# A two-layer Strassen kernel on one core: the first product in five groups of 464 token pairs instead of six of 384

## The chip, the core and the metric

The kernel runs on one core of a Trainium2 chip. The metric is the device time of one execution in microseconds, the median of several runs. Engines: TensorE (PE; its weight loads PEld), VectorE (DVE), ScalarE (ACT), GpSimd (POOL) and SyncE (SP), which here only issues DMAs.

## The reference

Chunked attention feeds two feed-forward layers in a row, all in float32:

```python
scores = scale * (q_c @ k_c.T)                 # chunks of 64 tokens, 8 heads of 64
x = softmax(scores) @ v_c                      # 4608 tokens x 512
h = x @ w_in;  s = h * softmax(h)              # first layer, 1024 wide
y = (layernorm(s) * g_ln) @ w_out              # 4608 x 512
h = y @ w_in2                                  # second layer, 2048 wide
g = max(h, 0) + alpha * min(h, 0)
out = g @ w_out2                               # 4608 x 512
```

## The kernel before

The first phase computes attention and the first layer for 36 tiles of 128 tokens, in an order written out by hand (`FIRST`, `STEP`, `LAST`), and stores `y` transposed to DRAM, one tensor `y_dram[s]` for each group of tokens (`ystore`, stores issued by SP, for the last two blocks by ACT).

The second phase, `phase2`, computes the second layer as two products, each with Strassen's scheme in its form of seven products of halves. Tokens go in pairs (first half, second half of a group), 2304 pairs in all. Each float32 operand is split into a high part (`high_y`, ACT) and a low part (`low_y`, DVE), and a product of halves takes three matmuls for each of two row blocks: six matmuls of one `w_in2` weight block each.

First product: six groups `s` of `SG` = 384 pairs, and for each group eight units `b`, one for each pair of 128 columns of the hidden layer. A unit runs the products p1, p6, p5, p7, p2, p3, p4, 42 matmuls with 384 columns. They go to four PSUM banks, x, y, z and v; p2, p3 and p4 add to the banks x, z and v after `s1` (ACT) has read x, `w` (DVE, output `wv`) has read z and `f("22")` has read v. Units take two sets of four banks in turn. DVE and ACT compute the four results of a unit (`f`, then `neg`, `pos`, and `end`, which together are the activation) and SP stores each, `g`, to DRAM (`gd`). The last three steps of a unit (`late`) are issued among the products of the next one.

The operands of the first product lie in 26 slots of one size on the left of SBUF. A group holds 14 while it runs: a high and a low part for each of seven products. During group `s` the next group is prepared: its four blocks of `y` are loaded at unit 1 (`load_y`, SP), the four sums are made by POOL at units 2 to 4 (`sum_y`), and the high and low parts follow at the places in `early`, `(unit, product)`: the low part always one product behind. A slot is taken from the top or from the bottom of the free ones, in turn by group. Where it stands in a unit: `extra(k)` is called after the k-th product has been issued with what reads it, so `(7, 1)` is in unit 7 behind p6 and what `late(2)` stores.

Second product: five chunks of pairs (`CHUNKS`); a chunk takes 28 steps of 12 matmuls, over four pieces `j`; first the products p1, p5, p6, p7 of all four pieces, then p2, p3, p4. A piece loads blocks a, b, c, d of `g` (`load_g`), and DVE and ACT make sums and parts (`prepare`, three steps ahead). Pieces 0 and 1 are prepared during the last group, in the same slots; their sums t4 go through DRAM. All later pieces use other buffers (`rp`, `op`, `hp`), which take over the slots' memory from the left end once the slots are given up (`ca.close()`). During the last group SP also loads the second product's weights, a quarter at a time (`load_w`).

Of the kernel before, what the change touches and what calls it, by code (L numbers as in the profile page):

```python
# [22 lines left out]
NT = B * S  # L23
# [10 lines left out]
SG = 384  # L34
NS = NT // (2 * SG)
PAIRS = NT // 2
NB2 = KF2 // 2
CHUNKS = [(0, 384), (384, 512), (896, 512), (1408, 512), (1920, 384)]
# [55 lines left out]
def tile_chunk_attention_solu_prelu(  # L94
# [24 lines left out]
    y_dram = [dram.tile([128, K1, 2 * SG], F32, name=f"yd{j}") for j in range(NS)]  # L119
# [49 lines left out]
    def phase1():  # L169
        with ExitStack() as c1, ExitStack() as c0:  # L170
# [394 lines left out]
            def ystore(j, m):  # L565
# [3 lines left out]
                for c, p in enumerate(pairs):  # L569
                    g, o = divmod(j * YG + p * YP, 2 * SG)  # L570
                    (nc.sync if j < YT + 3 else nc.scalar).dma_start(
                        out=y_dram[g][:, m, o:o + YP], in_=y[:, c * YP:(c + 1) * YP]
                    )
# [99 lines left out]
    def phase2():  # L673
        with ExitStack() as c2:
# [7 lines left out]
            tp = [P(f"t2{i}", 1, stack=ca) for i in range(26)]  # L682
# [13 lines left out]
            slots = list(range(26))  # L696
            homes, at = {}, [True]

            def slot(dtype, name, top=False):
                k = slots.pop(slots.index((max if top else min)(slots)))  # L700
                t = tp[k].tile([128, 2, SG], dtype, name=name, tag="t")
                homes[t.name] = k
                return t

            def free(t):
                slots.append(homes.pop(t.name))
# [3 lines left out]
            def load_y(s, which=YQ):  # L710
                at[0] = s % 2 == 0
                for t in which:
                    r, c = int(t[0]) - 1, int(t[1]) - 1
                    raw[t] = slot(F32 if t == "12" else F32R, f"y{t}", at[0])
                    nc.sync.dma_start(
                        out=raw[t].bitcast(F32), in_=y_dram[s][:, 2 * r:2 * r + 2, SG * c:SG * c + SG]
                    )

            def sum_y(k):
                out, a, b = (("t3", "22", "12"), ("t1", "12", "11"), ("t2", "22", "t1"), ("t4", "21", "t2"))[k]  # L720
                raw[out] = raw["12"] if out == "t1" else slot(F32, f"y{out}", at[0])
                for h in range(2):
                    sub(nc.gpsimd, *(raw[x][:, h].bitcast(F32) for x in (out, a, b)))

            def high_y(s, p):
                t = PRODUCTS[p][1]
                th[s, t] = slot(F32R, "th", at[0])
                copy(th[s, t], raw[t].bitcast(F32))

            def low_y(s, p):  # L730
                t = PRODUCTS[p][1]
                h, f = th[s, t], raw[t]
                l = slot(F32R, "tl", at[0]) if t[0] == "t" else f
# [5 lines left out]
            class Unit:  # L739


                def __init__(self, n, s, b):
                    self.s, self.b = s, b
                    self.ps = {x: ps2[n % 2].tile([128, SG], F32, name=f"h{x}", tag=f"b{x}") for x in "xyzv"}
# [16 lines left out]
                def tile(self, tag, where=None, bufs=1):  # L761
                    return (where or up).tile([128, SG], F32, name=tag, tag=tag, bufs=bufs)
# [33 lines left out]
                def store(self, t):  # L796
                    nc.sync.dma_start(out=GD[t][:, self.b, self.s * SG:self.s * SG + SG], in_=self.g[t])
# [331 lines left out]
```

## Time and profile before

| | |
|---|---|
| median of 3 runs | 1267.35 us (1267.33 to 1267.88) |
| profiled execution | 1267.81 us, of which the span in the trace is 1265.8 us |
| mean granted TensorE clock | 0.992 |
| PE busy | 1227.7 us (97% of the span), 8160 matmuls |
| DVE busy | 935.3 us (74%) |
| ACT busy | 682.5 us (54%) |
| POOL busy | 327.9 us (26%) |
| DMA | 237.89 MB, 188 GB/s on the mean |

The span runs from the first to the last instruction of the trace. Times in the rows are microseconds from the span's start unless marked ns. Matmuls overlap: one of 384 columns lasts 334 ns, but the next starts sooner, so the distance of starts is what counts. A wait is shown as the idle time of an engine and what ended it.

### The profile page before, as it was taken

The numbers are of one execution on the slowest core, as the hardware profiler recorded it, in microseconds if no ns is written. First come the engines' busy times: TensorE is split into PE (matmuls) and PEld (weight loads), VectorE is DVE, ScalarE is ACT, GpSimd is POOL, SyncE is SP. The second block draws the span as 40 slices with busy tenths as digits, with TensorE's granted clock in tenths as the row PEclk, the third lists the DMA queues.
The fourth block names the chain that finished last, engine by engine and source line by source line (L and its number), as shares of the span: only waits on it lengthen the run. The fifth ranks groups of instructions, "written<-read, shape, count | busy, mean of one in ns | idle before, by whom it ended". The sixth has DMA issues, their size and how long they took to land.

```text
span 1265.8 us, 21771 instructions
## 1 busy us (share of the span) xinstructions
PE 1227.7 (97%) x8160; PEld 1102.9 (87%) x8160; DVE 935.3 (74%) x1423; ACT 682.5 (54%) x1140; POOL 327.9 (26%) x309
## 2 busy tenths in 40 slices
PE   5789999999999999999999999999999999999998
PEld 4668888888888888879999999999989888888898
DVE  7986587777877777427878777777876959678584
ACT  6685455555556555436667666576534434434442
POOL 4665155535656545402020211200000000000000
PEclk8899999999999999999999999999999999999999
DMA  8443356554755633559444343428986648274462
GB/s 326 160 148 117 104 167 188 170 189 142 241 183 184 225 135 134 209 183 361 165 147 155 120 150 113 163 100 313 369 307 222 211 138 290 87 271 145 160 223 100
DMA packets 150409, 237.89 MB, mean 188 GB/s; under 512 B 15008, under 2 KB 100512, under 8 KB 149792
## 3 DMA queue, kind: packets, MB, share of 16 engines
q1 hardware_dynamic: 147840, 233.62, 53.9%
q10 hardware_dynamic: 2304, 2.10, 0.5%
q8 instruction: 64, 1.05, 0.3%
q0 software_dynamic: 160, 0.79, 0.1%
q14 instruction: 41, 0.34, 0.1%
HBM read 149.68 MB, written 86.77 MB: 187 GB/s over the span
## 4 chain that ended last, share of the span: by engine, by line
PE 47%; DMA 5%; DVE 1%; issue 0%; SPq 0%; ACT 0%; DVEq 0%; ACTq 0%
PE oz L986 7%; PE ov L986 7%; PE ox L986 7%; PE hz L753 7%; PE hv L753 6%; PE hx L753 6%; PE oy L986 3%; PE hy L753 3%; DMA w<-wod 3%; DMA rc<-gd 1%; DMA gd<-g 0%; DVE rt L668 0%; DVE rb L668 0%; DVE rlo L668 0%; DVE u L665 0%
## 5 line engine op out<-in xcount | busy, mean ns | idle before, releaser
L792 DVE SCALAR_TENSOR_TENSOR g<-ng,nal,g 128x384 f32<-128x384 f32 x192 | 124.1, 647 | 50.5 <-ACT g L671 50.5
L671 ACT ACTIVATE ng<-g 128x384 f32<-128x384 f32 x144 | 75.7, 526 | 119.1 <-DVE g L665 119.1
L165 PE MATMUL yps<-zz,wo_h 128*128 128x512 f32 x288 | 115.2, 400 | 0.8 <-ACT ysb L567 0.8
L753 PE MATMUL hv<-th,w 128*128 128x384 f32 x384 | 112.9, 334 | 1.5 <-DVE g L665 1.5
L753 PE MATMUL hz<-th,w 128*128 128x384 f32 x384 | 112.9, 334 | 0.1
L753 PE MATMUL hx<-th,w 128*128 128x384 f32 x384 | 112.8, 334 | 0.0
L167 PE MATMUL yps<-zz,wo_l 128*128 128x512 f32 x288 | 112.4, 390 | 0.0
L166 PE MATMUL yps<-zz,wo_h 128*128 128x512 f32 x288 | 112.2, 390 | 0.0
L986 PE MATMUL oz<-rhi,w 128*128 128x512 f32 (+1 forms) x304 | 93.9, 369 | 0.8 <-DVE osb L665 0.8
L986 PE MATMUL ox<-rhi,w 128*128 128x512 f32 (+1 forms) x304 | 93.8, 369 | 0.0
L986 PE MATMUL ov<-rhi,w 128*128 128x512 f32 (+1 forms) x304 | 93.7, 369 | 0.0
L668 POOL TENSOR_TENSOR yt<-y,y 128x384 f32<-128x384 f32 x24 | 28.2, 1194 | 235.4 <-DMA y<-yd 136.4
L671 ACT ACTIVATE rhi<-rt 128x1024 fp32r<-128x1024 f32 (+1 forms) x56 | 54.6, 984 | 60.7 <-PE oz L986 16.4
L671 ACT ACTIVATE g<-g 128x384 f32<-128x384 f32 x144 | 75.2, 522 | 3.1
L668 DVE TENSOR_TENSOR rlo<-rt,rhi 128x1024 fp32r<-128x1024 f32 (+1 forms) x56 | 62.3, 1125 | 15.2 <-ACT rhi L671 15.0
L753 PEld LDWEIGHTS hv<-th,w 128*128 128x128 f32 x384 | 70.7, 188 | 1.8 <-DVE g L665 1.8
L753 PEld LDWEIGHTS hz<-th,w 128*128 128x128 f32 x384 | 70.7, 188 | 0.4 <-DVE wv L665 0.4
L753 PEld LDWEIGHTS hx<-th,w 128*128 128x128 f32 x384 | 70.7, 188 | 0.0
L458 PE MATMUL h<-wi_h,xh 128*128 128x512 f32 x256 | 68.9, 391 | 0.0
L458 PE MATMUL h<-wi_l,xh 128*128 128x512 f32 x256 | 68.5, 389 | 0.0
L494 ACT ACTIVATE eh<-sl,st 128x1024 f32<-128x1024 f32 x36 | 41.4, 1151 | 45.5 <-DVE st L489 45.5
L167 PEld LDWEIGHTS yps<-zz,wo_l 128*128 128x128 f32 x288 | 54.0, 188 | 11.7
(179 smaller groups left out, 3270.4 us busy)
## 6 DMA issues: line engine op xcount, KB each, us to landing
gd<-g SPq DMA_DIRECT2D x192, 192.0 KB, 1.9
qkt<-in_qk SPq DMA_DIRECT2D x36, 512.0 KB, 5.6
w<-wod SPq DMA_DIRECT2D x28, 448.0 KB, 6.5
rc<-gd SPq DMA_DIRECT2D x24, 512.0 KB, 3.9
rd<-gd SPq DMA_DIRECT2D x24, 512.0 KB, 4.9
raw<-in_moe_w_out SPq DMA_DIRECT2D x24, 511.8 KB, 4.3
vt<-in_v SPq DMA_DIRECT2D x36, 256.0 KB, 4.5
y<-yd SPq DMA_DIRECT2D x24, 384.0 KB, 5.0
```

Source lines behind the costliest of these rows:

```text
L165: nc.tensor.matmul(o, lh, rh, start=first, stop=False)
L166: nc.tensor.matmul(o, lh, rl, start=False, stop=False)
L167: nc.tensor.matmul(o, ll, rh, start=False, stop=last)
L458: nc.tensor.matmul(ps[:, n], xh[:, kk], w[:, kk, 512 * n:512 * n + 512], start=(kk == 0 and w is wi_h), stop=False,)
L494: nc.scalar.activation(out=e, in_=s, func=AF.Square, bias=st[:, 4:5], accum_out=st[:, 5:6])
L668: eng.tensor_tensor(out=out, in0=a, in1=b, op=ALU.subtract)
L671: nc.scalar.activation(out=out, in_=in_, func=func, **k)
L753: nc.tensor.matmul(self.ps[x], w[:, a, i, k], d[:, k], start=(p not in CHAINED and k + j == 0), stop=(k == 1 and j == 2), skip_group_check ...
L792: nc.vector.scalar_tensor_tensor(out=self.g[t], in0=self.n[t], scalar=nal_sb[:, f:f + 1], in1=self.g[t], op0=ALU.mult, op1=ALU.add)
L986: nc.tensor.matmul(bank[key, m][:, :n], W[2 * j + k][:, a, i, 128 * m:128 * m + 128], d[:, k], start=(p not in CHAINED and j + k + q == 0) ...
```

## The change

The first product runs over five groups, four of 464 pairs and one of 448. A slot holds 464 columns and there are 24. Blocks 22 and 21 of `y` are given up once POOL's last sums have read them, and loaded again in unit 7, where the high and low parts of p2, p3 and p4 now stand two products later. The chunks of the second product are 464, 480, 480, 480 and 400 pairs wide, and its buffers 480. Piece 1 of the second product loads blocks c and d in unit 7. The t4 sums are stored by SP in place of POOL. The SBUF set aside for software DMA is given a size of its own, 512 B a partition. `y` stores are split where they cross a group's border.

```diff
 YP = 256
-SG = 384
-NS = NT // (2 * SG)
 PAIRS = NT // 2
+SG = 464
+GROUP = [(0, 464), (464, 464), (928, 464), (1392, 464), (1856, 448)]
+NS = len(GROUP)
+NSLOT = 24
 NB2 = KF2 // 2
-CHUNKS = [(0, 384), (384, 512), (896, 512), (1408, 512), (1920, 384)]
+CW = 480
+CHUNKS = [(0, 464), (464, 480), (944, 480), (1424, 480), (1904, 400)]
...
     b64 = const.tile([128, 2], F32, name="b64")
-    y_dram = [dram.tile([128, K1, 2 * SG], F32, name=f"yd{j}") for j in range(NS)]
+    y_dram = [dram.tile([128, K1, 2 * n], F32, name=f"yd{j}") for j, (_, n) in enumerate(GROUP)]
...
                 for c, p in enumerate(pairs):
-                    g, o = divmod(j * YG + p * YP, 2 * SG)
-                    (nc.sync if j < YT + 3 else nc.scalar).dma_start(
-                        out=y_dram[g][:, m, o:o + YP], in_=y[:, c * YP:(c + 1) * YP]
-                    )
+                    t0 = j * YG + p * YP
+                    for g, (p0, n) in enumerate(GROUP):
+                        a, b = max(t0, 2 * p0), min(t0 + YP, 2 * (p0 + n))
+                        if a < b:
+                            o = c * YP - t0
+                            (nc.sync if j < YT + 3 else nc.scalar).dma_start(
+                                out=y_dram[g][:, m, a - 2 * p0:b - 2 * p0], in_=y[:, a + o:b + o]
+                            )
...
             ca = c2.enter_context(ExitStack())
-            tp = [P(f"t2{i}", 1, stack=ca) for i in range(26)]
+            tp = [P(f"t2{i}", 1, stack=ca) for i in range(NSLOT)]
             wr = {}
...
-            slots = list(range(26))
+            slots = list(range(NSLOT))
             homes, at = {}, [True]
...
-            def slot(dtype, name, top=False):
+            def slot(dtype, name, top, n):
                 k = slots.pop(slots.index((max if top else min)(slots)))
-                t = tp[k].tile([128, 2, SG], dtype, name=name, tag="t")
-                homes[t.name] = k
+                t = tp[k].tile([128, 2, SG], dtype, name=name, tag="t")[:, :, :n]
+                homes[id(t)] = k, t
                 return t
...
             def free(t):
-                slots.append(homes.pop(t.name))
+                slots.append(homes.pop(id(t))[0])
...
                 at[0] = s % 2 == 0
+                n = GROUP[s][1]
                 for t in which:
                     r, c = int(t[0]) - 1, int(t[1]) - 1
-                    raw[t] = slot(F32 if t == "12" else F32R, f"y{t}", at[0])
+                    raw[t] = slot(F32 if t == "12" else F32R, f"y{t}", at[0], n)
                     nc.sync.dma_start(
-                        out=raw[t].bitcast(F32), in_=y_dram[s][:, 2 * r:2 * r + 2, SG * c:SG * c + SG]
+                        out=raw[t].bitcast(F32), in_=y_dram[s][:, 2 * r:2 * r + 2, n * c:n * c + n]
                     )
...
-            def sum_y(k):
+            def sum_y(s, k):
                 out, a, b = (("t3", "22", "12"), ("t1", "12", "11"), ("t2", "22", "t1"), ("t4", "21", "t2"))[k]
-                raw[out] = raw["12"] if out == "t1" else slot(F32, f"y{out}", at[0])
+                raw[out] = raw["12"] if out == "t1" else slot(F32, f"y{out}", at[0], GROUP[s][1])
                 for h in range(2):
                     sub(nc.gpsimd, *(raw[x][:, h].bitcast(F32) for x in (out, a, b)))
+                if s and k > 1:
+                    free(raw.pop(a))
...
                 t = PRODUCTS[p][1]
-                th[s, t] = slot(F32R, "th", at[0])
+                th[s, t] = slot(F32R, "th", at[0], GROUP[s][1])
                 copy(th[s, t], raw[t].bitcast(F32))
...
                 h, f = th[s, t], raw[t]
-                l = slot(F32R, "tl", at[0]) if t[0] == "t" else f
+                l = slot(F32R, "tl", at[0], GROUP[s][1]) if t[0] == "t" else f
                 sub(nc.vector, l, f.bitcast(F32), h.bitcast(F32))
...
                     self.s, self.b = s, b
-                    self.ps = {x: ps2[n % 2].tile([128, SG], F32, name=f"h{x}", tag=f"b{x}") for x in "xyzv"}
+                    self.p0, self.w_ = GROUP[s]
+                    self.ps = {
+                        x: ps2[n % 2].tile([128, SG], F32, name=f"h{x}", tag=f"b{x}")[:, :self.w_] for x in "xyzv"
+                    }
                     self.g, self.n = {}, {}
...
                 def tile(self, tag, where=None, bufs=1):
-                    return (where or up).tile([128, SG], F32, name=tag, tag=tag, bufs=bufs)
+                    return (where or up).tile([128, SG], F32, name=tag, tag=tag, bufs=bufs)[:, :self.w_]
...
                 def store(self, t):
-                    nc.sync.dma_start(out=GD[t][:, self.b, self.s * SG:self.s * SG + SG], in_=self.g[t])
+                    nc.sync.dma_start(out=GD[t][:, self.b, self.p0:self.p0 + self.w_], in_=self.g[t])
...
             for k in range(4):
-                sum_y(k)
+                sum_y(0, k)
             for p in PRODUCTS:
...
                 if x in pieces[:2]:
-                    return slot(dtype, f"f{tag}", True)
+                    return slot(dtype, f"f{tag}", True, n)
                 bufs = dict(t3=1, t2=1, t4=4, hi=4, lo=3).get(tag, 2)
-                return (hp if tag == "hi" else rp).tile([128, 2, 512], dtype, name=f"r{tag}", tag=tag, bufs=bufs)[:, :, :n]
-
-            def load_g(x):
+                return (hp if tag == "hi" else rp).tile([128, 2, CW], dtype, name=f"r{tag}", tag=tag, bufs=bufs)[:, :, :n]
+
+            def load_g(x, which="abcd"):
                 c, g, j = x
...
                 for tag, t in (("a", "11"), ("b", "12"), ("c", "22"), ("d", "21"))[2 * g:]:
+                    if tag not in which:
+                        continue
                     src[x, tag] = new(x, tag, F32 if tag == "b" else F32R)
...
                 free(d)
-                nc.gpsimd.dma_start(out=t4_dram[x[2]], in_=t4)
                 yield
+                nc.sync.dma_start(out=t4_dram[x[2]], in_=t4)
                 low6()
...
                     if x in pieces[:2]:
-                        nc.gpsimd.dma_start(out=t4_dram[x[2]], in_=t4)
+                        nc.sync.dma_start(out=t4_dram[x[2]], in_=t4)
                         done(t4)
...
                 def new_o():
-                    return op.tile([128, 512], F32, name="osb", tag="osb", bufs=2)[:, :n]
+                    return op.tile([128, CW], F32, name="osb", tag="osb", bufs=2)[:, :n]
...
                     if p == "p1":
-                        acc["u", m] = op.tile([128, 512], F32, name=f"u{m}", tag=f"u{m}")[:, :n]
+                        acc["u", m] = op.tile([128, CW], F32, name=f"u{m}", tag=f"u{m}")[:, :n]
                         copy(acc["u", m], x)
...
-            early = {(4, 1): "p1", (5, 1): "p6", (6, 1): "p5", (6, 2): "p7", (7, 1): "p2", (7, 2): "p3", (7, 3): "p4"}
+            early = {(4, 1): "p1", (5, 1): "p6", (6, 1): "p5", (6, 2): "p7", (7, 3): "p2", (7, 4): "p3", (7, 5): "p4"}
+            again = {(7, 1): ("21",), (7, 2): ("22",)}
             sums = {(2, 0): 0, (2, 3): 1, (3, 0): 2, (4, 0): 3}
...
                             if (b, k) == (6, 5):
-                                load_g(pieces[1])
+                                load_g(pieces[1], "ab")
+                            if (b, k) == (7, 1):
+                                load_g(pieces[1], "cd")
                             if b in (3, 4, 5, 6) and k in (2, 3):
...
                             if (b, k) in sums:
-                                sum_y(sums[b, k])
+                                sum_y(s + 1, sums[b, k])
+                            if (b, k) in again:
+                                load_y(s + 1, again[b, k])
                             if (b, k) in early:
...
         arrays["in_" + name] = a.view(np.int64) if a.dtype == np.float64 else a
-    nc = bacc.Bacc("TRN2", target_bir_lowering=False, num_devices=1)
+    nc = bacc.Bacc("TRN2", target_bir_lowering=False, num_devices=1, dynamic_dma_scratch_size=512)
     args = [
...
     r = run_bass_kernel_spmd(nc, [arrays], core_ids=[0])
-    o = r.results[0]["out_0"].reshape(DM, 2, NS, SG)
-    return np.ascontiguousarray(o.transpose(2, 1, 3, 0).reshape(NT, DM))
+    o = r.results[0]["out_0"]
+    return np.ascontiguousarray(np.concatenate([o[:, h, p:p + n] for p, n in GROUP for h in range(2)], axis=1).T)

```

## Rows read from the trace of the kernel before

**Rows 1.** Busy us by engine (instructions), granted clock, DMA share, GB/s, by stretch.

```profile
678.00:736.00 58.00, 58.00 (x337) 58.00 (x336) 45.35 (x80) 37.74 (x79) 9.11 (x8) 1.00 0.39 137
852.00:912.00 60.00, 60.00 (x348) 60.00 (x347) 47.85 (x85) 38.16 (x81) 0.76 (x1) 1.00 0.91 325
912.20:985.00 72.80, 68.94 (x379) 65.95 (x379) 52.40 (x61) 29.16 (x38) 0.55 (x1) 1.00 0.78 274
```

**Rows 2.** The chain that ended last, in order of time: start, us, what.

```profile
607.65 1.04 PE hy L753 x6
...
924.49 12.82 DMA rc<-gd
...
1000.12 2.72 PE oz L986 x12
```

**Rows 3.** Groups of instructions by form: busy us, mean ns of one, idle before.

```profile
L668 DVE TENSOR_TENSOR rlo<-rt,rhi 128x1024 fp32r<-128x1024 f32 x36 | 43.4, 1220 | 10.9 <-ACT rhi L671 10.9
L671 ACT ACTIVATE rhi<-rt 128x1024 fp32r<-128x1024 f32 x36 | 37.9, 1061 | 42.2 <-DVE rt L668 14.1 <-PE oz L986 11.8 <-PE oy L986 8.2
...
L665 DVE TENSOR_TENSOR wv<-hz,u 128x384 f32<-128x384 f32 x48 | 26.4, 549 | 0.4 <-PE hz L753 0.4
...
L671 ACT ACTIVATE th<-y 128x768 fp32r<-128x768 f32 x24 | 19.5, 837 | 3.0 <-DVE tl L668 2.1 <-ACT ysb L567 0.9
L668 DVE TENSOR_TENSOR tl<-yt,th 128x768 fp32r<-128x768 f32 x18 | 17.1, 953 | 13.1 <-ACT th L671 11.2 <-DMA yd<-ysb 1.3
...
L665 DVE TENSOR_TENSOR osb<-oz,u 128x512 f32<-128x512 f32 x12 | 7.7, 680 | 0.0
```

**Rows 4.** Timeline, from unit 7 of group 1 on: start, us, engine, instruction.

```profile
671.97 0.33 PE L753 MATMUL hx<-th,w 128*128 128x384 f32 x1
...
674.39 1.57 ACT L671 ACTIVATE th<-y 128x768 fp32r<-128x768 f32 x2
...
674.78 0.61 DVE L792 SCALAR_TENSOR_TENSOR g<-ng,nal,g 128x384 f32<-128x384 f32 x1
...
681.95 0.47 ACT L671 ACTIVATE s<-hx 128x384 f32<-128x384 f32 x1
...
683.46 0.55 DVE L665 TENSOR_TENSOR wv<-hz,u 128x384 f32<-128x384 f32 x1
...
687.44 0.32 SPq L797 DMA_DIRECT2D gd<-g  x1
...
687.87 0.37 SPq L715 DMA_DIRECT2D y<-yd  x1
```

**Rows 5.** Loads by tile: `y` in group 0, `rc` from 1100 to 1200.

```profile
L715 SPq DMA_DIRECT2D y<-yd x4: 371/398/482, 629.7 to 633.2; - x4
...
DMA to landing us min/median/max: 3.6/4.3/5.1
...
L892 SPq DMA_DIRECT2D rc<-gd x11: 359/360/466, 1100.6 to 1193.0; - x11
DMA to landing us min/median/max: 3.4/3.8/6.2
```

**Rows 6.** Timeline where the first product begins; waits stand in brackets.

```profile
547.46 0.60 ACT L567 ACTIVATE ysb<-yps 128x512 f32<-128x512 f32 x1 [7.22 <-DMA yd<-ysb]
...
552.26 0.50 PE L165 MATMUL yps<-zz,wo_h 128*128 128x512 f32 x1 [0.79 <-ACT ysb L567]
...
567.87 0.56 DVE L665 TENSOR_TENSOR g<-hv,wv 128x384 f32<-128x384 f32 x1 [3.42 <-DMA yd<-ysb]
...
568.49 0.44 PE L753 MATMUL hv<-th,w 128*128 128x384 f32 x1 [1.50 <-DVE g L665]
```

**Rows 7.** Timeline from the first product's end to the second chunk.

```profile
912.21 0.33 PE L986 MATMUL ox<-fhi,w 128*128 128x384 f32 x1
...
919.21 0.39 SPq L892 DMA_DIRECT2D ra<-gd  x1
...
978.08 0.47 PE L986 MATMUL oz<-rhi,w 128*128 128x512 f32 x1 [0.78 <-DVE osb L665]
```

## The prediction

> **What bounds the kernel now.** I read the page's busy shares first (the table above), then the table by stage, then the chain by order of time. TensorE is busy 97% of the span. In the middle groups of the first Strassen product it is busy 58.00 of 58.00 us, with VectorE at 45.35 and ScalarE at 37.74 [rows 1], so there only the number and the length of matmuls count. The chain says the same: six matmuls of 384 columns follow each other in 1.04 us and twelve of 512 in 2.72 us, without a break [rows 2]. TensorE loses time in few places: entering the first product, and between the two products. There, from 912.2 to 985, it is busy 68.94 of 72.80 us, and the chain runs through DMA: a load of `rc` took 12.82 us [rows 1, 2]. The last group moves 325 GB/s with the DMA engines at 0.91, against 137 and 0.39 in a middle one [rows 1].
>
> **Part 1, fewer and wider matmuls.** 1.04/6 is 173.3 ns for 384 columns, 2.72/12 is 226.7 ns for 512 [rows 2]. The difference of 53.3 ns over 128 columns is 0.417 ns a column, which leaves 13.3 ns per matmul whatever its width. A unit has 42 matmuls. Before there are 48 units, 2016 matmuls, 349.4 us. After, 32 units of 464 (206.7 ns) and 8 of 448 (200.0 ns) make 1680 matmuls: 1344 x 0.2067 + 336 x 0.2 = 345.0 us. That is **-4.5 us**. Bounds: if time went by columns alone the gain would be 0; two widths on one line leave no more than 4.5. The second product keeps five chunks, 336 matmuls each and 2304 columns: 0.
>
> The Trainium skill (TensorE: Matmul & The Clock Gate, Back-to-back issue gap) speaks against this: it gives the isolated gap as N/2.4 + 2.5 ns. By its fixed part 336 x 2.5 ns, about 0.8 us, would be gained, and the sum below would come out 3.7 us higher. The rows at two widths give 13.3 ns, and I go by them.
>
> **Part 2, the reloads at the group's end, the term that decides.** With 24 slots, y blocks 22 and 21 are freed after their sums and loaded again in unit 7, and the three last high/low splits move by two products. I carried unit 7 forward engine by engine, in the order of the code, with the trace's durations. Set at 384 columns this walk gives the trace of before: end of unit 6's 21 at 2.75 us after the unit's start (trace: 674.78 - 671.97 = 2.81), the next unit's first copy at 10.02 (9.98), its `wv` at 11.51 (11.49) [rows 4]. The widths scale by the two sizes of each form [rows 3]: a VectorE sum from PSUM 0.549 at 384 and 0.680 at 512, so 0.63; `end` 0.61 at 384 [rows 4], by the same slope 0.70; a low part 0.953 at 768 and 1.220 at 1024, so 1.12; a high part 0.837 and 1.061, so 0.98; the short ScalarE copies 0.55 to 0.58. Instructions of one engine overlap by some 0.09 (two high parts: 1.57 instead of 1.67).
>
> At 464 columns, from the unit's first matmul (a product is 1.24, a unit 8.68):
> SyncE can issue the reload of 21 only behind unit 6's last store, which waits for `end` of 21, done at 3.93. An issue follows the one ahead by some 0.42 (a store at 687.44, a y load at 687.87), so block 21 is issued at 4.39 and block 22 at 4.86. Landing: the quickest of a group's four y loads of 384 KB takes 3.6 us, `rc` of 512 KB, the first of a pair as block 21 is, 3.8 on the median [rows 5]; I take 3.7, so 21 lands at 8.09.
> ScalarE has done `neg` and `pos` of 22 at 7.05 and then stands at the high part of 21 until 8.13. Everything behind it is late by over a microsecond: `neg`/`pos` of 11 to 10.03, high of 22 to 10.92, `neg`/`pos` of 12 to 12.08, high of t4 to 12.97. VectorE follows: low of 21 to 10.27, sums and `end` to 11.43, low of 22 to 12.47, 21's sum to 13.03, low of t4 to 14.14, `end` of 12 to 14.74.
> The next unit's s1 copy ends at 14.11. Its fifth product, p2, accumulates into the bank that s1 reads and could start at 13.64: TensorE waits **0.52**. `u2`, `end` and `wv` follow on VectorE to 16.46; p3, which accumulates into the bank that `wv` reads, could start at 15.40: **1.10**. After that it catches up. (That such a bank wait is real the trace shows: 1.50 us before an `hv` matmul behind a VectorE read [rows 6].) Sum 1.62 per boundary; there are four, the last 0.15 dearer as the narrow group comes sooner to p2: **+6.6 us**. Bounds: with a landing of 2.5 or less, 0.46 remains from the splits' later place alone (+1.9); each further microsecond of landing is one more per boundary, and at the 5.1 that the slowest of the four y loads took it is 3.0 (+12).
>
> The Trainium skill (DMA: Bandwidth & Descriptors, Anatomy of one DMA) fits a transfer as 2.0 us + bytes/436 GB/s, from another issuing path; for 464 KB that estimate is 3.1 us. By it the term would be some +4.2 and the sum 2.4 us lower. The two rows at 384 and 512 KB, 3.6 and 3.8, lie above, and I keep 3.7.
>
> **Part 3, between the products.** The first product ends at 912.21; chunk 0 needs 28 x 12 x 173.3 ns = 58.24 and the first step of chunk 1 2.72, so its second step could start at 973.17. It starts at 978.08: 4.9 us lost [rows 7]. Behind it stand late loads: `ra` of piece 2 issued at 919.21, 7.0 after the product's end, landing among weights; and `rc` of piece 3, 12.82 [rows 2, 7]. After, chunk 0's step is 2.48 instead of 2.08, so step 8 comes 19.8 instead of 16.6 after the end, and the last group is 67.2 instead of 58.2 us long for the same weights, with DMA nearer 280 GB/s (325 x 58.2/67.2). But going through the slots by hand, piece 2's first buffer now lies on slot 0, which step 3 of piece 0 reads: its load can go at 9.92 + 0.2, some 10.1 after the end. Full DMA is some 357 GB/s (325/0.91); of the 3.6 us of a y load 1.1 are then transfer and 2.5 latency. So `rc`, the third of the loads, lands at 10.1 + 2.5 + 3.9 = 16.5; t3, the difference and the low part, 1.12 each, end at 19.9, just before the 20.05 at which the second matmul of step 8 wants it; behind t2 and t4 the low part of p5 ends at 23.1 and is wanted at 22.5: 0.6 late. With 0.3 for the boundary of chunks 0 and 1, 0.9 is lost instead of 4.9: **-4.0**. Bounds: -4.9 to +1 (if the load slips by as much as is won).
> Piece 1's blocks c and d are issued at unit 7 instead of unit 6, about 4 us before the end, and are wanted by VectorE some 3 after it: nothing, while they land within 7.
>
> **Part 4, entering the first product.** f22 stood 3.42 us for a store of `ysb` whose memory its output takes over, and TensorE 1.50 [rows 6]. With eight buffers of 1856 B the first `g` tile lies on the other, older `ysb` buffer, and the fourth product ends 0.8 later: -1.5. Against it: ScalarE waited 7.22 until 547.46 for a store behind the y and weight loads; these grow by 0.33 MB (0.8 us), and one low and two high parts in front of the next evacuation by some 0.4, so the wait at 552.26 grows by **+1.2** [rows 6]. Together **-0.3**, between -1.5 and +1.2.
>
> **At nothing.** 16 more y stores split at group borders (4 on ScalarE's queue, some 0.4 each, ahead of its wait for the loads). The four t4 transfers on SyncE: piece 0's stands behind a finished subtraction, piece 1's waits for VectorE at about 8 after the end, before the load that waits to 10.1 anyway; past 10.1 it would cost what it is late. POOL's wider sums: 9.11 us busy per group [rows 1], some 11 after, cover two units. 3.7 MB of reloads against 137 GB/s in use. The scratch and the 480-wide buffers set only addresses.
>
> **Sum.** -4.5 + 6.6 - 4.0 - 0.3 = -2.2. The profiled execution took 1267.8 us (span 1265.8), the median is 1267.35; I count from the median: **1265.1 us**. A measurement of this kernel tells 0.2%, 2.5 us, from no change: faster is below 1264.8, slower above 1269.9.
>
> **Rivals.**
> A: the boundaries cost little (0.46 each or less), because the reload lands before ScalarE comes to it. For: the walk leaves 2.66 us between the issue and ScalarE's arrival. Against: no row shows a landing below 3.4. Time 1267.35 - 8.8 + 1.9 = 1260.4. Chance 0.22.
> B: nothing is won between the products: the load waits for the slot and the splits follow late. For: the margin at step 8 is 0.15 us; against: less DMA traffic. 1265.1 + 4.0 = 1269.1. Chance 0.15.
> C, slower: the reloads land late. The loads share the queue with four stores per unit; `rc` took up to 6.2 [rows 5]. Without the boundaries the sum is -8.8; four waits reach the +11.3 that makes it slower when a landing takes 4.9 us. At 6.0 they are four times 3.92 and 0.15, and the time is 1274.4. Chance 0.11.
> D: wider matmuls bring nothing, 464 columns costing 464/384 of 173.3 ns: 1265.1 + 4.5 = 1269.6. Against it stand the two widths [rows 2]. The skill's 2.5 ns a matmul would come near to this. Chance 0.02.
> The forecast (a boundary at 1.2 to 2.1, 0.3 to 2 lost between the products) has 0.50, its own range 1262.5 to 1267.5; a little under half of it lies below 1264.8.
> Faster: 0.22 + 0.23 = 0.45. Same: 0.27 + 0.15 + 0.02 - 0.02 for B's upper tail = 0.42. Slower: 0.11 + 0.02 = 0.13. The range for 8 in 10 runs from 1260.0, A's with a little room, to 1269.5, which leaves out C and half of A's tail.
>
> **What would show it.** Six matmuls of a product in 1.24 us in groups 0 to 3 and 1.20 in group 4. At each of four boundaries a ScalarE wait of about 1.1 us on DMA before the high part of 21, then TensorE waits of 0.5 and 1.1 before `hx` and `hz` of the next group's first unit. No wait on `ysb` in the first unit; a wait of about 2 at the evacuation before. `ra` issued 10 us after the first product's end and TensorE waits below 1 us there. The prediction falls with the landing time of the reload: half a microsecond is 2 us of the result.

## The result: 1.1% slower, where a small gain was forecast

The changed kernel takes 1281.31 us (median of 4, 1279.66 to 1283.32), the kernel before in the same session 1267.62 (1267.33 to 1268.5). The ratio is 1.0108, 95% interval 1.009 to 1.0125. The forecast was 1265.1 with a range to 1269.5.

The profiled execution after took 1279.66 us (span 1277.9 against 1265.8, so 12.1 us to find). First its busy shares and the chain that ended last (start, us, what):

```profile
PE 1236.0 (97%) x7824; PEld 1075.9 (84%) x7824; DVE 929.9 (73%) x1344; ACT 676.2 (53%) x1061; POOL 325.7 (25%) x299
```

```profile
864.96 1.21 PE hv L766 x6
...
949.90 2.52 PE ov L1001 x12
...
995.24 2.62 PE oz L1001 x12
...
1212.70 2.19 PE ox L1001 x12
```

TensorE issues 336 matmuls fewer and is busy 8 us longer. The chain tells why, by the time from the start of one matmul to the start of the next: 1.21/6 is 202 ns at 448 columns, 2.52/12 is 210 at 464, 2.62/12 is 218.3 at 480, 2.19/12 is 182.5 at 400. My line through the two widths of [rows 2] says 200.0, 206.7, 213.3 and 180.0. The clock has no part in it. Here are the stretches of [rows 1] and one from the middle of the second product (PE, weight loads, DVE, ACT and POOL busy; granted clock; DMA):

```profile
678.00:736.00 58.00, 56.86 (x271) 50.31 (x270) 43.13 (x64) 36.50 (x66) 8.17 (x7) 1.00 0.43 152
852.00:912.00 60.00, 58.64 (x289) 53.71 (x288) 48.45 (x75) 37.74 (x70) 0.00 (x0) 1.00 0.86 306
912.20:985.00 72.80, 71.98 (x344) 64.09 (x343) 50.77 (x56) 30.88 (x39) 0.00 (x0) 1.00 0.75 268
1060.00:1205.00 145.00, 145.00 (x666) 124.66 (x665) 109.10 (x108) 58.94 (x64) 0.00 (x0) 1.00 0.56 186
```

The granted clock is 1.00 (2.4 GHz) in all four; before it was 1.00 in the same first three. TensorE lacks 1.1 and 1.4 us in the first two stretches, each of which holds the first unit of a group, where it lacked nothing before; in the third, which holds the passage between the products, it lacks 0.8 instead of 3.9. TensorE's waits over the whole execution (us in all, times, longest):

```profile
PE hz L766 <- DVE wv L672: 3.5, 4, 0.9
...
PE yps L168 <- ACT ysb L570: 2.9, 2, 1.5
...
PE hx L766 <- ACT s L678: 1.5, 4, 0.5
PE oz L1001 <- DVE rlo L675: 0.5, 1, 0.5
PE ox L1001 <- DVE ra L675: 0.4, 1, 0.4
```

One boundary in the timeline, from the reload to the two waits it was forecast to end in (compare [rows 4]):

```profile
630.07 0.92 SPq L723 DMA_DIRECT2D y<-yd  x2
...
633.98 0.98 ACT L678 ACTIVATE th<-y 128x928 fp32r<-128x928 f32 x1 [1.27 <-DMA y<-yd]
...
639.98 0.48 PE L766 MATMUL hx<-th,w 128*128 128x464 f32 x1 [0.38 <-ACT s L678]
...
642.39 0.48 PE L766 MATMUL hz<-th,w 128*128 128x464 f32 x1 [0.89 <-DVE wv L672]
```

And the entry, to set beside [rows 6]:

```profile
537.55 1.29 ACTq L578 DMA_DIRECT2D yd<-ysb  x3
...
550.30 0.60 ACT L570 ACTIVATE ysb<-yps 128x512 f32<-128x512 f32 x1 [8.32 <-DMA yd<-ysb]
...
550.95 0.50 PE L168 MATMUL yps<-zz,wo_h 128*128 128x512 f32 x1 [1.37 <-ACT ysb L570]
...
555.53 0.50 PE L168 MATMUL yps<-zz,wo_h 128*128 128x512 f32 x1 [1.52 <-ACT ysb L570]
...
563.87 0.37 PE L766 MATMUL hx<-th,w 128*128 128x464 f32 x1
```

Set against the forecast, term by term, from the starts of TensorE's matmuls in both traces (us):

| term | forecast | measured | how |
|---|---|---|---|
| first product's units | -4.5 | +0.2 | 32 x 8.80 + 8 x 8.505 against 48 x 7.28 |
| four boundaries | +6.6 | +7.1 | first units 10.60, 10.45, 10.56, 10.41 against 8.80 and 8.51 |
| between the products | -4.0 | -3.5 | lost 1.4 against 4.9 |
| entry | -0.3 | +0.3 | the first units' stalls gone, -2.2; from the fifth `y` evacuation ahead of the first `hx` to that `hx` 26.94 against 24.48, +2.5 |
| second product's matmuls | 0 | +6.7 | 336 x 20.0 ns: 209.6 + 3 x 218.3 + 182.2 against 2 x 173.3 + 3 x 226.7 |
| the end | 0 | +0.5 | |
| work ahead, unchanged | 0 | +0.8 | the same evacuation at 536.92 against 536.08 |

They add up to 12.1, the spans' difference. Two rows carry the miss, and both are the price of a matmul: 4.7 in the first product, 6.7 in the second.

### The profile page after: what moved, and what is told of

Same layout as the page of the kernel before. It is cut to its first block, busy times and chain, and to the rows that moved or that the text cites. A ratio compares the mean times of both kernels' runs of the same rounds, so it can differ in the third digit from the quotient of the medians.

```text
span 1277.9 us, 20839 instructions
## 1 busy us (share of the span) xinstructions
PE 1236.0 (97%) x7824; PEld 1075.9 (84%) x7824; DVE 929.9 (73%) x1344; ACT 676.2 (53%) x1061; POOL 325.7 (25%) x299
## 5 line engine op out<-in xcount | busy, mean ns | idle before, releaser
L805 DVE SCALAR_TENSOR_TENSOR g<-ng,nal,g 128x464 f32<-128x464 f32 (+1 forms) x160 | 118.7, 742 | 46.9 <-ACT g L678 43.6
L678 ACT ACTIVATE ng<-g 128x464 f32<-128x464 f32 (+1 forms) x120 | 70.8, 590 | 126.2 <-DVE g L672 125.6
L766 PE MATMUL hz<-th,w 128*128 128x464 f32 (+1 forms) x320 | 105.8, 371 | 3.5 <-DVE wv L672 3.5
L766 PE MATMUL hx<-th,w 128*128 128x464 f32 (+1 forms) x320 | 105.8, 371 | 1.5 <-ACT s L678 1.5
L766 PE MATMUL hv<-th,w 128*128 128x464 f32 (+1 forms) x320 | 105.3, 370 | 0.0
L1001 PE MATMUL ov<-rhi,w 128*128 128x480 f32 (+2 forms) x304 | 94.4, 371 | 0.0
L1001 PE MATMUL ox<-rhi,w 128*128 128x480 f32 (+2 forms) x304 | 94.4, 371 | 0.0
L1001 PE MATMUL oz<-rhi,w 128*128 128x480 f32 (+2 forms) x304 | 94.4, 371 | 0.0
L675 DVE TENSOR_TENSOR rlo<-rt,rhi 128x960 fp32r<-128x960 f32 (+2 forms) x56 | 62.0, 1114 | 20.5 <-ACT rhi L678 20.4
L678 ACT ACTIVATE g<-g 128x464 f32<-128x464 f32 (+1 forms) x120 | 70.4, 586 | 2.6
```

The lines of the kernel that those rows point to most:

```text
L675: eng.tensor_tensor(out=out, in0=a, in1=b, op=ALU.subtract)
L678: nc.scalar.activation(out=out, in_=in_, func=func, **k)
L766: nc.tensor.matmul(self.ps[x], w[:, a, i, k], d[:, k], start=(p not in CHAINED and k + j == 0), stop=(k == 1 and j == 2), skip_group_check ...
L805: nc.vector.scalar_tensor_tensor(out=self.g[t], in0=self.n[t], scalar=nal_sb[:, f:f + 1], in1=self.g[t], op0=ALU.mult, op1=ALU.add)
L1001: nc.tensor.matmul(bank[key, m][:, :n], W[2 * j + k][:, a, i, 128 * m:128 * m + 128], d[:, k], start=(p not in CHAINED and j + k + q == 0) ...
```

## Experiments: is it the width, or where the operand lies?

In the changed kernel the width of a matmul, the distance between the rows of its operand in SBUF and all addresses move together. Theory W puts the cost down to the width, theory P to the place (the row distance), theory S to the smaller scratch, which shifts the addresses. Four kernels separate them. **Only the widths** of the second product, tiles still 512 columns wide:

```
-CHUNKS = [(0, 384), (384, 512), (896, 512), (1408, 512), (1920, 384)]
+CHUNKS = [(0, 384), (384, 480), (864, 480), (1344, 480), (1824, 480)]
```

> The kernel before, with only the second product's chunks changed to 384 and four of 480 columns; its tiles stay 512 columns wide, so each row of a tile still begins 2048 bytes behind the one ahead. The same 2304 columns in the same 1680 matmuls. My line through 384 and 512 (13.3 ns plus 0.417 ns a column) says 213.3 ns for 480: the second product keeps its length, 1267.4 us, within 1 us. Theory W (a width of 480 itself costs more, as the changed kernel's 218.3 ns show): 1344 matmuls x 5.0 ns = +6.7 us, 1274. Theory P (not the width but the distance of the rows, 1920 or 1856 bytes, costs it): 213.3 ns and no change.

Measured 1271.79 us, ratio 1.0027 (1.0017 to 1.0038). **The same with tiles 480 columns wide:**

```
-... .tile([128, 2, 512], dtype, name=f"r{tag}", tag=tag, bufs=bufs)[:, :, :n]
+... .tile([128, 2, 480], dtype, name=f"r{tag}", tag=tag, bufs=bufs)[:, :, :n]
```

> As the run ahead of it (chunks of 384 and four of 480 columns in the kernel before), but with the second product's tiles 480 columns wide, so that the second row of a tile begins 1920 bytes behind the first and every second tile begins off a multiple of 2048. Theory W: 218.3 ns a matmul as with wide tiles, about 1274 us. Theory P: 218.3 ns here against 213.3 in the wide tiles; 1274 here and 1267.4 there. The last theory left, that the smaller scratch shifts all addresses, S: 213.3 ns in both, since the scratch is the old one.

One execution, 1275.07 us. The chain of the first and then of the second:

```profile
982.92 2.60 PE ov L986 x12
```

```profile
983.92 2.62 PE ov L986 x12
```

2.60/12 is 216.7 ns in wide tiles, 2.62/12 is 218.3 in narrow ones, on the line it would be 213.3. So of the 5.0 ns that 480 columns miss, 3.4 are the width and 1.6 the tile. Neither theory alone holds, and S falls, since the scratch is the old one in both. In the first of the two 1344 x 3.4 ns is 4.6, and 1.6 us less were lost between the products (3.3 instead of 4.9): 3.0 expected from these, 3.5 measured.

**Five widths in one run,** `CHUNKS = [(0, 384), (384, 448), (832, 464), (1296, 496), (1792, 512)]`, wide tiles:

> The kernel before with the second product's chunks at 384, 448, 464, 496 and 512 columns, tiles 512 wide: five widths in one run, each 336 matmuls. The line says 173.3, 200.0, 206.7, 220.0 and 226.7 ns. Theory W expects the changed kernel's 202.4 at 448 and 209.6 at 464, and some 3 to 5 above the line at 496; theories P and S expect the line at all five.

One execution, 1272.84 us. Theory W holds at each (chain; 448, 464, 496, 512 columns):

```profile
984.84 2.43 PE ov L986 x12
...
1045.64 2.51 PE ox L986 x12
...
1115.83 2.68 PE ox L986 x12
...
1193.78 2.72 PE oz L986 x12
```

**The even pieces undone** in the changed kernel:

```
-CW = 480
-CHUNKS = [(0, 464), (464, 480), (944, 480), (1424, 480), (1904, 400)]
+CW = 512
+CHUNKS = [(0, 384), (384, 512), (896, 512), (1408, 512), (1920, 384)]
```

> The changed kernel with the second product's chunks put back to 384, 512, 512, 512, 384 and its tiles to 512 columns: the even pieces undone, the rest kept. Theory W: the three chunks of 480 and those of 464 and 400 lose their excess, some 6.9 us, and the time is 1274.4. Theory P: the same but for chunk 0, whose 384 columns lie in slots with rows 1856 bytes apart and would still be 2 to 3 ns over 173.3, some 0.8 us: 1275.2. If neither holds and the excess comes with the smaller scratch (S), 512 columns take more than 226.7 ns here and little is won: 1280 to 1282.

Measured 1277.8 us, ratio 1.0073 (1.0058 to 1.0088): 3.5 below the changed kernel, not 6 to 7. The matmuls are back at 173.3 to 173.8 and 226.7 ns, all 6.7 us of them. But with chunk 0 at 384 the loss between the products is 5.0 instead of 1.4, with `ox` waiting 2.7 us for `ra` (0.4 in the changed kernel). So the wide chunk 0 does what Part 3 says, and the other chunks spoil it. This loss varies from trace to trace: 1.4 to 3.0 in four kernels here whose chunk 0 has 464 columns, 3.3 to 6.7 in those with 384.

**Which widths?** Two more runs in wide tiles, `CHUNKS = [(0, 384), (384, 256), (640, 320), (960, 352), (1312, 288), (1600, 240), (1840, 464)]` and `CHUNKS = [(0, 384), (384, 504), (888, 416), (1304, 432), (1736, 368), (2104, 200)]`. By then 304 columns had been seen at 137.5 ns (below), and 384, 464 and 480 lie on one proportion, rival D's:

> The kernel before with the second product in chunks of 384, 256, 320, 352, 288, 240 and 464 columns, tiles 512 wide: seven widths, 336 matmuls each. Three laws through what has been seen. Q, proportional, 0.4514 ns a column: 256 115.6, 320 144.4, 352 158.9, 288 130.0, 240 108.3, 464 209.4 ns. L, 13.3 ns plus 0.417 a column: 120.0, 146.7, 160.0, 133.3, 113.3, 206.7. W, the line at multiples of 128 and some 3 ns more elsewhere: 120.0, 149.7, 163.0, 136.3, 116.3, 209.7. The early sight of 304 columns at 137.5 (Q 137.2, L 140.0, W 143.0) speaks for Q.

> The kernel before with the second product in chunks of 384, 504, 416, 432, 368 and 200 columns, tiles 512 wide. Q (0.4514 ns a column): 504 227.5, 416 187.8, 432 195.0, 368 166.1, 200 90.3 ns. L (13.3 + 0.417 a column): 223.3, 186.7, 193.3, 166.7, 96.7. If 504 takes 227 ns or more, 512 at 226.7 stands alone off the proportional law; if it takes 223 to 225 the law bends towards the line above 480.

One execution each (1285.56 and 1278.34 us; more chunks load more weights). The chain of the first at 256, 320 and 288 columns, and of the second at 504, 416 and 200:

```profile
980.00 1.44 PE ov L986 x12
...
1023.33 1.76 PE ov L986 x12
...
1122.11 1.58 PE ox L986 x12
```

```profile
982.12 2.72 PE ov L986 x12
...
1050.12 2.26 PE ox L986 x12
...
1236.88 1.34 PE oz L986 x12
```

All widths in tiles 512 wide, ns from start to start (typical step of 12; 304 from the run with both repairs):

| columns | 200 | 240 | 256 | 288 | 304 | 320 | 352 | 368 | 384 |
|---|---|---|---|---|---|---|---|---|---|
| measured | 111.7 | 111.7 | 120.0 | 131.7 | 137.5 | 146.7 | 160.8 | 166.7 | 173.3 |
| line | 96.7 | 113.3 | 120.0 | 133.3 | 140.0 | 146.7 | 160.0 | 166.7 | 173.3 |

| columns | 416 | 432 | 448 | 464 | 480 | 496 | 504 | 512 |
|---|---|---|---|---|---|---|---|---|
| measured | 188.3 | 195.0 to 196.7 | 202.5 | 209.2 to 210.0 | 216.7 | 223.3 | 226.7 | 226.7 |
| line | 186.7 | 193.3 | 200.0 | 206.7 | 213.3 | 220.0 | 223.3 | 226.7 |

Q falls (256 is 120.0, not 115.6), and so does W as I had put it (320 and 368 are on the line, 288 and 304 under it). What is left is plainer: the line holds from 240 to 384 within 2.5 ns, from 416 to 504 a matmul takes 1.6 to 3.4 ns more, and 504 takes as long as 512, which is on the line again. The change put its chunks and groups into that stretch.

**Does the place count in the first product too?** Slots 480 wide under the 464 columns, and slots 432 wide under the 384 of the kernel before (with the small scratch for room):

```
-t = tp[k].tile([128, 2, SG], dtype, name=name, tag="t")[:, :, :n]
+t = tp[k].tile([128, 2, 480], dtype, name=name, tag="t")[:, :, :n]
```

> The changed kernel with slots 480 columns wide instead of 464, so that rows lie 1920 bytes apart and a slot begins every 3840 bytes instead of 3712; nothing else. Theory W (the width alone): the spacing at 464 stays at 208.3 to 210 in all products. Theory P (where the slot lies): the products at 213.3 move, or the mean of 209.6 changes by 1 ns or more, up or down: 1 ns is 1.3 us in the first product.

> The kernel before with the small DMA scratch and slots 432 columns wide for its 384, rows 1728 bytes apart, a slot every 3456 bytes instead of 3072. Theory W: 173.3 ns in every product. Theory P: some products take 175 to 178, since a slot then no longer begins at a multiple of 1024 bytes; at 2 ns over all the first product grows by 4 us.

One execution each. With slots of 480 the mean at 464 is 209.4 instead of 209.6 and the units stay at 8.80, 1281.5 us in all. But in slots of 464 the products of the first group take from 207.0 to 213.0 ns a matmul, each the same in unit after unit, and in slots of 480 all take 209.2 to 209.8: place moves single products by some 3 ns either way and leaves the mean at 464 almost alone. With slots of 432 the 384 columns take 174.4 ns on the mean, units 7.31 to 7.35 behind the first, and 1269.92 us: 48 x 0.045 is 2 us. So the place counts by 0.2 to 1.6 ns on the mean, the width by 2 to 3. The two do not settle the last nanosecond: at the same width and row distance 464 columns took 208.9 ns in one run and 210.0 in another, and 400 took 182.2 in the changed kernel and 183.3 in the one with early reloads. Why stays open.

## Experiments: the boundaries

The reloads are issued earlier, and the splits are back where they were:

```
-early = {..., (7, 3): "p2", (7, 4): "p3", (7, 5): "p4"}
-again = {(7, 1): ("21",), (7, 2): ("22",)}
+early = {..., (7, 1): "p2", (7, 2): "p3", (7, 3): "p4"}
+again = {(6, 4): ("21",), (7, 0): ("22",)}
```

> The changed kernel with the reload of block 21 moved from unit 7 to unit 6 (behind its fifth product) and that of 22 to the start of unit 7, and the three last high/low splits put back to where the kernel before has them; 24 slots suffice for that. Theory of the late reload (the 7.0 us at four boundaries come from ScalarE standing at block 21 and the splits being late): the first unit of each group is again as long as the others, 8.80 instead of 10.4 to 10.6, and the time falls by 7 us, from 1281.3 to 1274.3. Rival (the boundary costs what three splits on wider tiles cost, wherever the reload stands): 0.5 us or more stay at each boundary, 1276 to 1281. The spacing of the matmuls stays as in the changed kernel (209.6, 202.5, 218.3 ns).

Measured 1275.45 us, ratio 1.0055 (1.0041 to 1.0068), 5.9 less than the changed kernel. The first units of the groups last 9.07, 8.86, 8.83 and 8.79 us against 8.79 to 8.83 and 8.52: 0.6 left of 7.1. ScalarE still waits for the loads, 11.2 us in four (4.9 in four in the changed kernel), yet the first units are short again. The reloads and the splits moved together here, so how the 6.5 divide between them is not shown. The profiled execution is 4.3 us shorter and not 6.5, since between the products it lost 3.0 instead of 1.4.

**Both repairs:** the early reloads, `CW = 512`, and chunk 0 left wide:

```
+CHUNKS = [(0, 464), (464, 512), (976, 512), (1488, 512), (2000, 304)]
```

> The early reloads of the run ahead of it, and the second product in chunks of 464, 512, 512, 512 and 304 columns with tiles 512 wide: chunk 0 stays wide, three chunks get a width that runs at 226.7 ns, only two widths are odd. If the two losses are separate they add up: the second product's matmuls take 70.4 + 228.5 + some 48 (304 columns at 0.417 ns and 16 ns) = 346.9 us instead of 351.6, so 4.7 less than the early reloads alone, 1269.6 us; the waits between the products stay near 1.3, since the wide chunk 0 stays. If the wide chunk 0 is not what keeps those waits short (the undone chunks of 384 had 5.0 us of them), they come back here too and the time is 1273.

Measured 1267.83 us, ratio 0.9999 (0.999 to 1.0008): 13.5 below the changed kernel and even with the kernel before. The matmuls of the second product take 336 x (209.2 + 3 x 226.7 + 137.7) = 345.1 us, 6.6 less than in the changed kernel, and 2.2 are lost between the products.

## Experiments: entry and the stretch between the products

Part 3 put the kernel before's loss down to late loads of piece 2, Part 4 its first unit's stall to a store of `ysb`. In the kernel before, the small scratch makes room for four buffers of their own for piece 2:

```
+nc = bacc.Bacc("TRN2", ..., dynamic_dma_scratch_size=512)
+xq = P("x2", 1, side="right")
 gp = P("g2", 1, side="right", stack=ca)
...
+if x == pieces[2] and tag in "abcd":
+    return xq.tile([128, 2, 384], dtype, name=f"q{tag}", tag=tag)
...
+if (b, k) == (5, 5):
+    load_g(pieces[2])
...
-load_g(pieces[2])
```

> The kernel before with the small DMA scratch, whose freed memory holds the four loads of piece 2 in buffers of their own; they are issued in unit 5 of the last group instead of after the first product. Theory: the 4.9 us between the products of the kernel before come from these loads being late behind their memory and the weights; then 1 us or less is left and the time is 1267.6 - 4 = 1263.6. Rival: what is late is the memory of the split's results or the loads of piece 3, and the waits only move to step 12 of the chunk: 1266 to 1268.

With `yp = R("y", 3)` in place of 2 besides:

> As the run ahead of it, with a third buffer for the evacuation of y. Theory: ScalarE's 7.2 us wait for a store of y (8.3 in the changed kernel) is what delays the last evacuations and so the first product's start; with a third buffer the wait is gone, TensorE's 0.8 us before the evacuations too, and the first unit's stall behind a store may go: 0.8 to 2.3 us less than the run ahead of it. Rival: the wait is covered, since ScalarE then only meets the y loads and the high parts later; no difference within 1 us.

The first takes 1266.03 us, ratio 0.9984 (0.9976 to 0.9993); the second 1267.81, 1.0001 (0.9992 to 1.001). In the first the rival's 1266 holds and the theory's 1263.6 does not. The third buffer removes ScalarE's 7.2 us wait for a store and gains nothing: the first `hx` starts 0.8 sooner, and the second and fourth units are then 0.8 and 0.7 longer, with waits of 0.3 before `hz`. Its theory falls, and at 1.8 us above the run ahead of it the rival's "within 1 us" does too. Two controls, the scratch alone, and the extra buffers with the loads put back behind the product:

> The kernel before with the small DMA scratch alone. It shifts the addresses of the left-hand buffers by 15872 bytes, a multiple of 512. Theory (it only sets addresses): no change, within 1 us of the kernel before, the first unit still 9.1 us long behind the store of y, the spacing 173.3 and 226.7. Rival: the shift moves the stall of the first unit or the waits between the products by 1 to 2 us either way.

> As the run that loaded piece 2 early, with its extra buffers, but the four loads of piece 2 back behind the first product. Theory of the addresses: the first unit is 7.3 us as there (the g tile no longer lies over the last y buffer), the waits between the products stay near 4 us, and the time is that run's within 0.7 us, some 2 below the kernel before. Rival, the loads: the waits between the products are 1 us or more longer than with the early loads, and the time is 1 us or more above that run.

The scratch alone: 1268.1, ratio 1.0007 (0.9998 to 1.0017), no difference that can be told, though its trace lost 6.7 us between the products. The buffers without the early loads: 1265.93, ratio 0.9988 (0.9978 to 0.9997). TensorE's waits in that run and then with the early loads, behind the first product:

```profile
929.61 0.44 PE L989 MATMUL ox<-qa,w 128*128 128x384 f32 x1 [2.24 <-DVE qa L668]
932.34 0.44 PE L989 MATMUL oz<-rlo,w 128*128 128x384 f32 x1 [0.36 <-DVE rlo L668]
```

```profile
933.45 0.44 PE L989 MATMUL oz<-rlo,w 128*128 128x384 f32 x1 [1.39 <-DVE rlo L668]
```

The early loads remove the wait at the piece they bring, and most of it stands again one step on, at a split's low part: 5.4 lost without them, 4.0 with them. Most of the 1.4 between the two is paid at another place, the last unit of the first product, which takes 8.50 us with the early loads and 7.28 without. There VectorE waits for a store of `g`, and TensorE behind it:

```profile
909.77 0.56 DVE L665 TENSOR_TENSOR g<-hv,wv 128x384 f32<-128x384 f32 x1 [2.69 <-DMA gd<-g]
910.39 0.44 PE L753 MATMUL hv<-th,w 128*128 128x384 f32 x1 [0.93 <-DVE g L665]
```

So there is no difference in the time. The gain of both runs is at the entry: their first unit lasts 7.3 us instead of 9.1, as the extra buffers push `g` off the memory of the y store. With the scratch alone `hv` still waits 1.57 us there.

## Experiment: groups at the cheap widths

If 384 and 512 are cheap, groups of these two should bring what 464 did not. 23 slots of 512 columns fit, with four `g` buffers instead of six:

```
+SG, NSLOT, CW = 512, 23, 512
+GROUP = [(0, 384), (384, 512), (896, 512), (1408, 512), (1920, 384)]
+CHUNKS = [(0, 512), (512, 512), (1024, 512), (1536, 384), (1920, 384)]
...
+early = {(4, 1): "p1", (5, 1): "p6", (6, 1): "p5", (7, 0): "p7", (7, 2): "p2", (7, 3): "p3", (7, 4): "p4"}
+again = {(6, 4): ("21",), (7, 0): ("22",)}
...
-self.g[t] = self.tile("g", gp, 6)
+self.g[t] = self.tile("g", gp, 4)
...
-low7()
-free(t3)
-free(t4)
+free(t4)
+low7()
+free(t3)
```

Piece 1 also loads its blocks a and b at two places instead of one.

> The changed kernel with groups of 384, 512, 512, 512 and 384 pairs, the second product in chunks of 512, 512, 512, 384, 384; 23 slots 512 wide, four buffers for g instead of six, p7's split one step later, blocks 21 and 22 loaded again in unit 6 and at the start of unit 7. No group border cuts a y store any more. Theory Q (a matmul takes 0.4514 ns a column, 384/173.3, at every width run so far but 512, which alone is cheap at 226.7): first product 24 units x 42 x 226.7 + 16 x 42 x 173.3 = 345.0 us against 349.4 before and 350.6 with the early reloads, boundaries 1 us or less each, no third wait for split stores: 1267.8 - 5.6 + 2 - 1 = 1263. Rival: with 23 slots and four g buffers the engines stand in turn, and what the width gives is lost at the boundaries and in the units: 1266 to 1269.

Measured 1287.29 us, ratio 1.0155 (1.0141 to 1.0169): nearer the rival, and 18 us above its range too. The units of 512 do run in 9.52 us, 42 x 226.7 ns, with 0.4 to 0.7 at a boundary; those of 384 take up to 11.36, and the last one 14.09. TensorE's waits:

```profile
PE hx L766 <- ACT s L678: 6.2, 4, 4.1
PE hv L766 <- DVE g L672: 5.8, 7, 2.4
PE hz L766 <- DVE wv L672: 3.2, 8, 0.9
```

Behind them VectorE waits 15.0 us for stores of `g`. TensorE's longest wait, 4.1 at `hx` in the last unit, has another cause. The edit frees `t4` ahead of p7's low part, `flo`, and a `flo` waits for the store of `t4` (in the changed kernel one such wait of 1.4; the early freeing was not run by itself):

```profile
920.79 1.23 DVE L675 TENSOR_TENSOR flo<-ft,fhi 128x1024 fp32r<-128x1024 f32 x1 [5.43 <-DMA t4d<-ft]
925.00 0.69 PE L766 MATMUL hx<-th,w 128*128 128x384 f32 x1 [4.10 <-ACT s L678]
```

With the order of widths changed to 512, 384, 512, 384, 512:

> As the run with groups of 384, 512, 512, 512, 384, but in the order 512, 384, 512, 384, 512. There the 512-column units ran at 9.52 us without a wait and the boundaries between them cost 0.4 to 0.7; the loss of 20 us lay in the two groups of 384, the first and the last, where the weights are loaded and four buffers for g wait for their stores. Theory of the stores: with 512 columns in the two loaded groups the waits go, the first product takes 345.0 and 2 to 3 us for boundaries, its start some 2 later than in that run for the larger y loads: 1264 to 1266. Rival: four buffers are too few at either width under that traffic, or 384 columns stall in the quiet groups too: 1270 or more.

Measured 1275.26 us, ratio 1.0057 (1.0042 to 1.0071). The 384-wide groups, now in the quiet middle, have units of 7.85 to 8.80 us in half of their places, `hz` waits nine times in all (3.5 us), VectorE still waits 9.4 us in seven for stores of `g` in the first product (a wait that the changed kernel, with six buffers, does not show), and the first product starts at 564.41, as a first group of 512 loads more ahead of it (560.50 with a first group of 384; ScalarE's wait for the y store 9.0 us). The last unit takes 11.09 instead of 9.52, and `flo` waits 4.1 us for the store of `t4` there. The rival's time holds, 1270 or more. Its reason, too few `g` buffers, is shown in part: two of the seven waits, 5.3 us, fall in the 384-wide groups, in units of 8.80 and 7.85, and for the other slow units it is not shown. Six buffers beside slots of 512 were not run. The kernel before with the shifted buffers stays the fastest version, 1.4 us under the kernel before without the early loads and 2.2 with them, both barely clear of the noise.

## Why the prediction was wrong, step by step

- **Part 1 failed, twice: the price of a matmul at a width that no row showed.** "The difference of 53.3 ns over 128 columns is 0.417 ns a column" is an interpolation between two widths that both happen to be cheap: 464 takes 209.6 ns, not 206.7. The gain of 4.5 became a loss of 0.2, just past the part's own other bound (nothing gained). And "the second product keeps five chunks, 336 matmuls each and 2304 columns: 0" priced by columns what moves off 512: 6.7 us. No bound was set for that zero, although no row of before shows 400 or 480. Together 11.4 of the 14.3 us between the forecast -2.2 and the measured 12.1.
- **Rival D** gave 464 columns 209.4 ns and had a chance of 0.02. Its number was right by luck, its law was not (256, 320 and 368 columns lie on the line), and it too left the second product out.
- **The Trainium skill** (TensorE: Matmul & The Clock Gate, Back-to-back issue gap) gives N/2.4 + 2.5 ns for the isolated gap. The traces here, with a weight load for every matmul, disagree at every width: the part above N/2.4 is 10.8 at 304, 13.3 at 256, 384 and 512, 16.7 at 480.
- **Part 2 was right.** Waits at `hx` and `hz` of each first unit, ScalarE standing 1.27 us at block 21, the first reload 3.9 us from its issue to ScalarE's start; 7.1 instead of 6.6, of which the waits at `hx` and `hz` make up 5.0. The run with early reloads, its splits moved back with them, shows that their places were the cause.
- **Part 3 was right in size (-3.5 for -4.0),** with `ra` issued 10.5 us after the product's end, and chunk 0's width is what brings it (384 gives the loss back); from trace to trace this term moves by over 1 us. But that the kernel before loses this time to late loads is only the first of two things: with the loads early the splits are late, and the last unit of the first product pays for the loads.
- **Part 4:** the first unit's stall went as told (-2.2 for -1.5). The other half was 2.5 for 1.2. The split stores, costed at nothing, lie on ScalarE's queue (0.81 us became 1.29, twice) ahead of the store that it waits for. An estimate gives them some 0.8; no run has them alone. The run whose first group of 512 cuts no store takes 27.15 from evacuation to `hx`, 2.67 over before for 128 columns more. In proportion the 80 more of 464 are worth 1.7 by their larger loads, and 0.8 of the 2.5 is left.
- **Rival C** named the right sign for a reason that did not come: the first reload took 3.9 us to ScalarE's start, not the 4.9 and more that the rival needed.

What in TensorE makes 416 to 504 columns dearer than the line stays open; the runs show the size and where it begins and ends, not the cause.

## What to carry to other kernels

Price an operation at a size that the trace has, or set a bound for the size: two sizes do not show that those between lie on a line, and an unchanged total of columns is no price of zero. On these runs, with fp32 matmuls back to back, 384 and 512 columns are good widths and 400 to 504 are not. A second load that saves memory cost 0.6 us in four boundaries, and not 7.1, when it was issued a unit earlier and the work behind it was not pushed back for it. With both repairs the wider groups come out even with the kernel before, not ahead of it.

## What the runs showed of the hardware

- A matmul of 504 columns takes as long as one of 512 (226.7 ns), and between 416 and 504 each takes 1.6 to 3.4 ns more than a line that holds at 256, 320, 368, 384 and 512.
- 200 and 240 columns take the same 111.7 ns a matmul; between these two the width does not set the time.
- Where the moving operand lies costs too: 480 columns 216.7 ns in rows 2048 bytes apart and 218.3 at 1920; 384 columns 173.3 at 1536 and 174.4 on the mean at 1728. Some 1 ns a matmul also differs between runs of one width and row distance (464 columns 208.9 and 210.0; 400 columns 182.2 and 183.3).
